# A delta-rule recurrence feeding a two-layer MLP: triangular inverses in 16x16 blocks, joined by small TensorE products

## The chip, the cores and the metric

The kernel runs on one core of one Trainium2 chip. The metric is the device time of one execution in microseconds (us), as a median of several executions. Engines are named as the profile names them: PE is TensorE (matrix products), PEld its weight loads, DVE is VectorE, ACT is ScalarE, POOL is GpSimd, SP issues DMAs. "Fast" and "slow" are the two states that executions fall into; only fast ones are compared.

## The reference, cut to what matters

```python
# q, k, v, beta, g: batch 4, 8 heads, 768 tokens, head size 48
k_n = k / (norm(k) + 1e-6)
for t in range(S):
    y[t] = g[t] * (q[t] @ state)                  # read before the update
    state += beta[t] * outer(k_n[t], v[t] - k_n[t] @ state)
h = x @ w_in                                      # x = y, 3072 tokens x 384; w_in 384 x 2048
out = softplus(h) @ w_out                         # w_out 2048 x 384
```

The recurrence is worked in chunks of 64 tokens. Within a chunk the update is a triangular system, (I + beta L) u = beta (v - k S), with L the strictly lower part of k k^T. The kernel inverts its diagonal blocks and multiplies.

## The kernel before: the parts that matter here

The whole program is a list of items with an engine, a cost estimate, dependencies and a priority. A small planner simulates the engines and emits the instructions in the order that it finds, so each engine has a fixed queue. There are six super-steps (`cc`) of 128 tokens. Each has a preparation (norms, transposes, k k^T, the inverse), a recurrence (two chunks in sequence) and the MLP ("MoE" below) of 512 rows.

```python
# the inverse: one 32x32 block per lane (128 lanes), column by column, on GpSimd
def step(eng, tr_, j, c0, c1, nn=nn, tt=tt):
    n, w = HC - 1 - j, c1 - c0                    # HC = 32: 31 dependent steps
    tmp = tr_.ap[:, : n * w].rearrange("p (i c) -> p i c", c=w)
    eng.tensor_tensor(tmp, nn.ap[:, j+1:, j:j+1].broadcast_to([P, n, w]),
                      tt.ap[:, j:j+1, c0:c1].broadcast_to([P, n, w]), ALU.mult)
    eng.tensor_tensor(tt.ap[:, j+1:, c0:c1], tt.ap[:, j+1:, c0:c1], tmp, ALU.add)
# ... cut: in super-step 0 the columns are split between DVE and GpSimd ...
nc.scalar.copy(t16.ap, tt.ap)                                          # to fp16
nc.vector.transpose(td.ap.rearrange("p u i -> p i u"), t16.ap)         # to TensorE's layout

# k k^T, per head and half: three small products, each with its own weights
nc.tensor.matmul(o[ra, :, h, :], ka, x.ap[r, h, 0, :])
nc.tensor.matmul(o[rb, 0, h, :], kb_, kb_)
nc.tensor.matmul(o[rb, 1, h, :], kb_, ka)

# the inverse applied: 32x32 products, first for all four quarters, then again for two
for h in range(H):
    for qd in parts:                              # (0, 1, 2, 3), later (1, 3)
        r = slice(32 * qd, 32 * qd + 32)
        nc.tensor.matmul(hd(up.ap)[r, h], td_.ap[r, gi * H + h, :], o.ap[r, h])
```

Each `matmul` call becomes two PE instructions, a weight load and a product.

## Time and profile before

| | before |
|---|---|
| time, median | 397.4 us |
| products on PE | 6088 |
| PE busy | 258.4 us |
| GpSimd busy | 235.2 us |
| first recurrence with an inverse | 75.2 us |
| first MoE product | 111.7 us |

Busy time is what an engine executes, whether or not anybody waits for it. The chain of waits is read from the last instruction backwards and says what set the end: half of it is GpSimd. The prediction below shows these lines and reads them. It is the queue of DMAs that bring instructions (number, megabytes, share of 16 DMA engines' time):

```profile
q8 instruction: 47, 0.77, 0.8%
```

0.77 MB in 47 transfers is 16 KB each.

### The profile page before, as it was taken

The numbers are of one execution on the slowest core, as the hardware profiler recorded it, in microseconds if no ns is written. First come the engines' busy times: TensorE is split into PE (matmuls) and PEld (weight loads), VectorE is DVE, ScalarE is ACT, GpSimd is POOL, SyncE is SP. The second block draws the span as 40 slices with busy tenths as digits, with TensorE's granted clock in tenths as the row PEclk, the third lists the DMA queues.
The fourth block names the chain that finished last, engine by engine and source line by source line (L and its number), as shares of the span: only waits on it lengthen the run. The fifth ranks groups of instructions, "written<-read, shape, count | busy, mean of one in ns | idle before, by whom it ended". The sixth has DMA issues, their size and how long they took to land.

```text
span 395.2 us, 13701 instructions
## 1 busy us (share of the span) xinstructions
PE 258.4 (65%) x6088; PEld 163.3 (41%) x6088; DVE 184.8 (47%) x344; ACT 133.5 (34%) x224; POOL 235.2 (60%) x396
## 2 busy tenths in 40 slices
PE   0052100387598169599699648889549999289985
PEld 0042100376543147364266235665225654056442
DVE  1141898969420388651464059742065540254011
ACT  0331001363436243416521357332434217211630
POOL 2440484428888938888888874888813888400000
PEclk9999999999999759959899959898955999779999
DMA  3699876156650046462045031253000010011002
GB/s 71 118 184 183 154 144 119 39 108 123 121 104 0 13 95 130 84 121 53 2 97 125 24 61 27 55 114 72 9 2 3 23 48 14 2 30 34 22 20 61
DMA packets 108634, 27.71 MB, mean 70 GB/s; under 512 B 103072, under 2 KB 108192, under 8 KB 108576
## 3 DMA queue, kind: packets, MB, share of 16 engines
q1 hardware_dynamic: 105216, 23.61, 30.5%
q0 software_dynamic: 2464, 3.15, 4.7%
q8 instruction: 47, 0.77, 0.8%
q10 hardware_dynamic: 896, 0.10, 0.2%
q14 instruction: 11, 0.09, 0.1%
HBM read 25.26 MB, written 4.72 MB: 76 GB/s over the span
## 4 chain that ended last, share of the span: by engine, by line
POOL 51%; DVE 19%; PE 16%; issue 9%; ACTq 3%; DMA 1%; ACT 1%; POOLq 0%; DVEq 0%
POOL tt L544 22%; POOL tmp L538 20%; POOL ss L335 6%; PE o L856 6%; DVE td L617 5%; PE h L824 4%; DVE tmpv L538 3%; DVE tt L544 3%; ACTq L235 3%; POOL nn L511 2%; DVE ln L499 2%; PE d L388 2%; DVE kn L352 1%; DVE ss L322 1%; DVE mt L481 1%
## 5 line engine op out<-in xcount | busy, mean ns | idle before, releaser
L538 POOL TENSOR_TENSOR tmp<-nn,tt 128x31 f32<-128x31 f32 (+23 forms) x178 | 87.7, 493 | 33.1 <-DVE nn L511 19.3
L544 POOL TENSOR_TENSOR tt<-tt,tmp 128x31 f32<-128x31 f32 (+23 forms) x178 | 92.9, 522 | 13.9
L856 PE MATMUL o<-w_out,ga 128*128 128x384 f16 x384 | 81.4, 347 | 9.4 <-ACT ga L838 6.4
L824 PE MATMUL h<-xt,w_in 128*128 128x512 f16 x288 | 78.0, 407 | 2.7 <-DVE xt L778 1.3
L838 ACT ACTIVATE ga<-h 128x512 f16<-128x512 f32 x96 | 56.8, 597 | 64.1 <-PE h L824 62.0
L335 POOL TENSOR_TENSOR ss<-ss,half_c 128x16 f32<-128x16 f32 x12 | 35.0, 2920 | 31.3 <-DVE ss L322 31.2
L856 PEld LDWEIGHTS <-ga 128*128 128x128 f16 x384 | 36.4, 102 | 36.5 <-issue 8.1
L667 PE MATMUL d<-w,td 32*32 32x48 f16 x1152 | 19.3, 193 | 48.6 <-DVE ss L342 37.2
L388 PE MATMUL d<-ident,kn 64*64 64x64 f16 x384 | 14.1, 230 | 51.2 <-DVE kn L352 50.8
L824 PEld LDWEIGHTS <-w_in 128*128 128x128 f16 x288 | 28.0, 101 | 38.9 <-issue 14.4
L676 ACT CAST u<-d 128x384 f16<-128x384 f32 x48 | 21.9, 481 | 59.1 <-PE d L667 59.0
L617 DVE STREAM_TRANSPOSE td<-t 128x1024 f16<-128x1024 f16 x6 | 27.9, 4646 | 28.1 <-ACT t L608 28.1
L667 PEld LDWEIGHTS <-td 32*32 32x32 f16 x1152 | 14.6, 98 | 57.2 <-DVE ss L342 37.5
L408 ACT COPY kqt<-d 128x1024 f16<-128x1024 f16 x24 | 23.7, 1012 | 33.3 <-PE d L388 33.2
L388 PEld LDWEIGHTS <-kn 64*64 64x64 f16 x384 | 11.5, 142 | 53.6 <-DVE kn L352 52.8
L659 DVE TENSOR_TENSOR w<-vf,d 128x384 f16<-128x384 f32 x48 | 25.5, 546 | 13.2 <-PE d L684 12.3
L342 DVE TENSOR_SCALAR ss<-ss 128x16 f32<-128x16 f32 x12 | 3.7, 307 | 59.0 <-POOL ss L335 59.0
L869 DVE COPY osb<-o 128x384 f32<-128x384 f32 x24 | 13.5, 564 | 34.4 <-PE o L856 34.4
L481 DVE TENSOR_TENSOR mt<-d,mask 128x512 f16<-128x512 f32 x24 | 16.0, 685 | 19.6 <-PE d L461 19.4
L309 ACT ACTIVATE ksq<-kf 128x384 f32<-128x384 f32 x24 | 12.0, 522 | 34.6 <-DMA kf<-in_k_dram 31.0
L511 POOL TENSOR_TENSOR nn<-ln,nbeta_l 128x1024 f32<-128x1024 f16 x5 | 9.6, 1913 | 15.2 <-DVE ln L499 15.1
L444 ACT CAST kk<-d 128x512 f16<-128x512 f32 x24 | 13.6, 588 | 14.3 <-PE d L428 14.3
(54 smaller groups left out, 362.9 us busy)
## 6 DMA issues: line engine op xcount, KB each, us to landing
kf<-in_k_dram SPq DMA_DIRECT2D x48, 96.0 KB
qf<-in_q_dram SPq DMA_DIRECT2D x48, 96.0 KB
vf<-in_v_dram SPq DMA_DIRECT2D x48, 96.0 KB
gf<-in_g_dram SPq DMA_DIRECT2D x48, 96.0 KB
out_dram<-osb SPq DMA_DIRECT2D x48, 96.0 KB
w_in<-in_moe_w_in_dram POOLq DMA_DIRECT2D x1, 1536.0 KB, 11.3
w_out<-in_moe_w_out_dram POOLq DMA_DIRECT2D x1, 1536.0 KB, 21.7
beta_l<-in_beta_dram ACTq DMA_DIRECT2D x16, 6.0 KB
```

Source lines behind the costliest of these rows:

```text
L335: nc.gpsimd.tensor_tensor(ss.ap, ss.ap, half_c, ALU.pow)
L388: nc.tensor.transpose(o[r, h, j, :], a.ap[r, h, :], ident[r, r])
L408: lambda tp=tp, o=kqt[gi]: nc.scalar.copy(o.ap.rearrange("p h j t -> p (h j t)"), f16ps(tp.ap))
L538: eng.tensor_tensor(tmp, nn.ap[:, j + 1 :, j : j + 1].broadcast_to([P, n, w]), tt.ap[:, j : j + 1, c0:c1].broadcast_to([P, n, w]), ALU.mult,)
L544: eng.tensor_tensor(tt.ap[:, j + 1 :, c0:c1], tt.ap[:, j + 1 :, c0:c1], tmp, ALU.add)
L617: lambda t16=t16, td=td: nc.vector.transpose(td.ap.rearrange("p u i -> p i u"), t16.ap)
L659: nc.vector.tensor_tensor(o.ap, vf.ap, hd(wp.ap), ALU.subtract)
L667: nc.tensor.matmul(hd(up.ap)[r, h], td_.ap[r, gi * H + h, :], o.ap[r, h],)
L676: nc.scalar.copy(o.ap, hd(up.ap))
L824: nc.tensor.matmul(hp.ap, w_in[:, j, f * P : (f + 1) * P], xt.ap[:, j, :], start=(j == 0), stop=(j == 2),)
L838: lambda hp=hp, o=gb_: nc.scalar.activation(o.ap, hp.ap, AF.Softplus)
L856: nc.tensor.matmul(op.ap[:, :DM], ga[f].ap[:, 128 * gi : 128 * gi + 128], w_out[:, f, :], start=(f == 0), stop=(f == NF - 1),)
```

## The change

The intent is to take the inverse off the critical path. Blocks of 16x16 need 15 steps instead of 31 and a quarter of the elements. The lower left quarter of each 32x32 inverse is then made by TensorE: T21 = -T22 L21 T11. The transpose to TensorE's layout is done in fp32 with contiguous writes. Loads of the inputs are twice as large and half as many, beta is loaded by GpSimd's queue instead of ACT's, and the first super-step takes its square roots on ACT. The pairing of batches and the priorities of the items change too.

```diff
-        def step(eng, tr_, j, c0, c1, nn=nn, tt=tt):
-            n, w = HC - 1 - j, c1 - c0
+        def step(j, tmp=tmp, nn=nn, tt=tt, eng=eng):
+            n, w = 15 - j, j + 1
+            t = tmp.ap[:, : 2 * n * w].rearrange("p (b i c) -> p b i c", b=2, c=w)
             eng.tensor_tensor(...)               # both 16x16 blocks of a lane in one instruction
...
+        def ttr(t32=t32, tt=tt):                 # fp32 transposes, contiguous output
+            for b in range(2):
+                c0 = 16 - 16 * b
+                nc.vector.transpose(
+                    t32.ap[:, 16 * b : 16 * b + 16], tt.ap[:, b, :, c0 : c0 + 32])
...
+        def nat(...):                            # T11 transposed back: 128 products
+            for u in range(U):
+                for qd in range(4):
+                    r = slice(32 * qd, 32 * qd + 32)
+                    nc.tensor.matmul(uv(np_.ap)[r, u], td.ap[r, u, :],
+                                     ident[r, 32 * qd : 32 * qd + 16])
+        def xmm(...):                            # L21 T11: 128 products
+                    r = slice(32 * qd, 32 * qd + 16)
+                    nc.tensor.matmul(uv(xp.ap)[32 * qd : 32 * qd + 32, u],
+                                     kk.ap[r, 0, u, :], tn.ap[r, u, :])
+        def tmm(...):                            # add -T22 X: 4 + 128 products
+                    nc.tensor.matmul(uv(ep.ap)[32 * qd : 32 * qd + 16, u],
+                                     xs.ap[r, u, :], td.ap[r, u, 16:], start=False, ...)
...
-    r_k = ring("kf", 4, [P, H, D], F32)
+    r_k = ring("kf", 3, [P, 2, H, D], F32)      # loads of 192 KB instead of 96 KB
...
-                    nc.scalar.dma_start(out=beta_l[l0 : l0 + 8], ...)      # 16 of them
+                nc.gpsimd.dma_start(out=beta_l[l0 + cl : l0 + 32 : 2], ...)  # 8
...
-        pl = 100 * cc - 200                      # preparation
+        pl = 100 * cc - 70
```

## The prediction

> **What bounds the kernel now.** I read the page first (busy shares, tenths, chain of waits), then the busy time by stretch, then the timelines of GpSimd and of the first 76 us, then the TensorE instructions one by one.
>
> The page, busy time and the chain that ended last:
>
> ```profile
> PE 258.4 (65%) x6088; PEld 163.3 (41%) x6088; DVE 184.8 (47%) x344; ACT 133.5 (34%) x224; POOL 235.2 (60%) x396
> ...
> PE   0052100387598169599699648889549999289985
> ...
> POOL 2440484428888938888888874888813888400000
> PEclk9999999999999759959899959898955999779999
> ...
> POOL 51%; DVE 19%; PE 16%; issue 9%; ACTq 3%; DMA 1%; ACT 1%; POOLq 0%; DVEq 0%
> ```
>
> PE has the most busy time, yet the chain runs for half of the span on GpSimd. The groups of instructions say with what (count, busy us, mean ns):
>
> ```profile
> L538 POOL TENSOR_TENSOR tmp<-nn,tt 128x31 f32<-128x31 f32 (+23 forms) x178 | 87.7, 493 | 33.1 <-DVE nn L511 19.3
> L544 POOL TENSOR_TENSOR tt<-tt,tmp 128x31 f32<-128x31 f32 (+23 forms) x178 | 92.9, 522 | 13.9
> ...
> L335 POOL TENSOR_TENSOR ss<-ss,half_c 128x16 f32<-128x16 f32 x12 | 35.0, 2920 | 31.3 <-DVE ss L322 31.2
> ...
> L617 DVE STREAM_TRANSPOSE td<-t 128x1024 f16<-128x1024 f16 x6 | 27.9, 4646 | 28.1 <-ACT t L608 28.1
> ```
>
> There are six super-steps of 128 tokens. Each needs the triangular inverses of 128 blocks of 32x32, one to a lane: 31 dependent column steps of two instructions. In the GpSimd timeline the inverses of super-steps 1 to 5 start at 94, 150, 190, 248 and 305 us and the last ends at 341.8: some 50 us apart, of which one inverse is 37.7 (94.1 to 132.0), the two powers 5.8, the scaling of N 1.9 and clearing T 1.2, together 46.6. So the middle is GpSimd-bound. Two more parts are not: a head, until super-step 0 has gone through the recurrence, and a tail after 341.8. Busy time by stretch (window, length, then PE, PEld, DVE, ACT, POOL with counts, clock, DMA share, GB/s):
>
> ```profile
> 0.00:42.00 42.00, 9.81 (x416) 8.64 (x416) 11.15 (x38) 9.05 (x13) 11.66 (x17) 1.00 0.84 144
> 42.00:75.00 33.00, 0.00 (x0) 0.00 (x0) 30.84 (x70) 2.52 (x4) 21.45 (x49) 1.00 0.60 114
> ...
> 303.00:342.00 39.00, 34.32 (x532) 18.89 (x528) 11.11 (x23) 11.96 (x22) 33.99 (x63) 0.94 0.09 22
> ```
>
> In the second stretch PE does nothing: the first inverse runs, split between DVE and GpSimd (44 to 68.6), then a 1.0 us cast and the 4.6 us transpose. The first recurrence starts at 75.2 and the first MoE product only at 111.7 (timeline of PE). The first 14 us look like this:
>
> ```profile
> 0.81 12.36 ACTq L235 DMA_DIRECT2D beta_l<-in_beta_dram  x16
> ...
> 14.49 1.76 ACT L309 ACTIVATE ksq<-kf 128x384 f32<-128x384 f32 x4
> ```
>
> The first half of k had landed at 5.5 us (k is the first 4096 packets of the SP queue; the 2048th ended there), but ACT was issuing beta loads until 13.2.
>
> **What the Trainium skill says.** (1) "GPSIMD Engine Reference", section 3.1 Elementwise: a two-input elementwise instruction costs software dispatch plus about 2.6 cycles per element. The trace agrees in form: a line through 183 start-to-start times of the column steps gives 0.281 us plus 1.82 ns per element. Halving the work therefore does not halve the fixed part unless the count falls too. (2) "TensorE: Matmul & The Clock Gate", Part 3, The mechanism: 32x32 tiles of the array overlap, a few ns apart. The trace agrees: 64 products of 32x32 (w,td) take 0.83 us at half clock and 32 take 0.38 us at full, so about 9 ns each. (3) The same page, "What's actually happening": an idle window of about 3.4 us drops the clock to half. The trace agrees: after the idle 283 to 289 us three h products take 1.46 us, against 0.81 warm. A PE with fewer idle gaps will also be a faster PE. (4) "ScalarE: Activation LUTs", What ACT_TABLE_LOAD costs: 1283 ns; the two loads here show exactly 1283. The new Sqrt in super-step 0 adds a switch.
>
> **The change part by part.**
>
> *Inverse on GpSimd.* Blocks shrink to 16x16, two to a lane and both in one instruction: 15 steps, 30 instructions, with 2 x sum of (15-j)(j+1) = 1360 elements each for multiply and add, 2720 in all. By the line above: 30 x 0.281 + 2720 x 0.00182 = 8.4 + 5.0 = 13.4 us (the same line gives 37.3 for the old form, measured 37.7). Two preps of 256: 1.5 us. Clear and diagonal: about 0.8. One power over 32 columns instead of two over 16: 5.8, unchanged, as it scales with columns (2.92 for 16). Sum 21.5 us against 46.6 per super-step. GpSimd falls to about 5 x 21 plus the start, some 120 us: no bound.
>
> *First inverse, all on DVE.* The DVE steps of the old one fit 0.178 us + 2.1 ns per element: 30 x 0.178 + 2720 x 0.0021 = 11.1 us, against 24 now. Saves 13 in the head.
>
> *Transpose.* One fp16 transpose with scattered 2-byte writes, 4.65 us, becomes two fp32 ones of 512 elements with contiguous output. The ln transpose, with contiguous output, is 1.9 us for 1024 elements, so at most 1 us each; I take 1.4 for both. DVE loses 3.2 us per super-step, 20 in all. The ACT cast stays, 1.05.
>
> *The join, new.* nat 128, xmm 128, tmm 132 products per super-step. At 9 ns: 1.2 + 1.2 + 1.4 = 3.8 us of PE, 23 us over six, and three ACT evictions of 512 columns at about 0.59 (as the kk row) = 1.8 us, 11 us over six. As latency: 1.4 + 1.05 + (1.4 + 0.6) x 2 + 1.6 + 0.6 and some 1.2 of hand-overs = 10 us, about what cast, transpose and waits take now (66 or 68.6 to 75.2).
>
> *Loads.* Same bytes, same 192 B packets, half the issues: no bandwidth gained, and the DMA share is low after 112 us. Beta leaves ACT for GpSimd: eight software DMAs at about 1 us (the two weight loads show 0.97 and 1.19). They stand ahead of the identity on GpSimd, and the DVE queue starts with the identity cast, then the memsets. So the first reduce waits until about 12.5 instead of 15.6: a gain of 3, not 8. Sqrt on ACT replaces two 2.9 us powers there.
>
> *Head, added up.* First reduce 12.5; sqrt, reciprocal, scale: first kn at about 15.5 and second at 17 (20.6 and 26.1 now). Transposes, kqt and kk copies (ACT 4 x 1.0 + 4 x 0.59 = 6.4) and the "issue" gaps of PE under heavy DMA load (3.2 and 4.2 us now, I keep about 5): kk complete near 30 (40.4 now). ln 1.9, preps 0.8, steps 11.1: 44. Join 10: the recurrence starts at about 54, against 75.2. The recurrence of a super-step alone took 19 us late in the trace (347.6 to 366.5), 36 in the head, where it waited for powers and k of the next; I take 22. The first MoE product starts at about 76, against 111.7: **36 us gained in the head.**
>
> *After the head PE is the bound.* Work at full clock: MoE 288 x 0.216 + 384 x 0.163 = 124.8 us (medians of the start-to-start times). Small products: the 64-row ones at 16.5 ns, the 32-row ones at 9 to 10, transposes of y at 66: 73.9 us. Join 23. Total 222, of which prep 0 and 1, recurrence 0 and join 0, 5 + 5 + 7.6 + 3.8 = 21, fall into the head. Left: 201 us. No stretch runs at 100%: by the same accounting 305 to 337 us had 0.87 of its time in such work, 248 to 282.5 had 0.79, 194 to 227 had 0.75, each with a full queue of MoE work but half-cold clock in the latter two. With the clock warm more often I take 0.85: 201 / 0.85 = 236. The last copy and store add 2 to 3. Sum: 76 + 236 + 2 = **314 us.**
>
> **The rivals.** (a) *GpSimd still bounds*: the 16x16 steps cost more than the line says, as every access now has one more dimension. At double, 27 + 8 = 35 us per super-step, still below PE's 37 / 0.85 = 43. Time 320 to 330. Speaks against: the line fits short and long steps alike. (b) *The chain through the join bounds*: k, norm, power 5.8, transposes, ln, 15 us of GpSimd, 10 us of join is some 45 us per super-step, with five PSUM banks shared by prep, join and recurrence. If it isn't overlapped with the super-step before, PE idles and cools as now: 340 to 365. For it: in-order queues planned from estimates, five banks only. Against: k, kn and kqt have room for more than two super-steps, and preparation has only to fit into gaps of PE. (c) *DVE or ACT bound*: DVE falls to 185 - 13 - 20 + some 5 = 157, ACT rises to 145; both are half of 314, so no. (d) *The MoE tail and the recurrence chain are denser than I think*: at 0.92, 218 us, time 296.
>
> **Range and chances.** Density 0.78 to 0.92 moves the sum by about plus or minus 20; the head by plus or minus 8. Range 292 to 338. For the change to stay within 2%, 83 us of gain would have to vanish although GpSimd's half of the chain is cut by more than half: 2% for same, 1% for slower, 97% for faster.
>
> **What would show it right or wrong.** GpSimd steps: 30 per super-step, about 13.4 us from first to last; GpSimd busy near 120 us. First recurrence product near 54 us and first MoE product near 76. Join: PE bursts of 128 in about 1.2 us. The two fp32 transposes below 1 us each. The chain of waits led by PE, with GpSimd below 15%; PE busy above 75% of the span; mean clock above 0.92. Wrong: if the chain still names GpSimd, or if PE shows gaps over 3 us in the middle that wait on td or on a PSUM bank (rival b); if beta or the identity holds DVE past 15 us; or if a strided ACT copy or the fp32 transposes take several us.

## The result, and the profile after

The changed kernel takes 363.6 us (median of 4 executions, 362.6 to 369.7; the longest is a slow one, and the three fast ones have the median 363.0), against 397.4. The ratio is 0.914, with a 95% interval of 0.911 to 0.917. Ratios here are the mean time of one kernel's fast runs over that of the other's in the same rounds, so they are not quite the ratio of the medians quoted. It is faster, as forecast, but by 34 us and not by 83; 363.6 lies well outside 292 to 338.

The page of the changed kernel, in the same rows as before:

```profile
PE 274.1 (76%) x8416; PEld 175.7 (49%) x8416; DVE 148.1 (41%) x280; ACT 148.9 (41%) x233; POOL 104.5 (29%) x196
...
PE   0351035669996897779999978985899978999984
...
POOL 6400060054830892000528987000006600000000
PEclk9985555555997599569999998995599998999999
...
q8 instruction: 65, 1.06, 1.3%
...
PE 71%; issue 13%; DVE 7%; ACT 5%; SPq 2%; DMA 1%; DVEq 0%; ACTq 0%
```

GpSimd has left the chain altogether, and PE carries it, as predicted. Two entries don't fit. "issue", time in which an engine waited for nothing that the profile shows, is 13% of the chain, 47 us. And the clock row has a long stretch of fives, half clock, near the start, where the kernel before had nines. The groups behind the prediction's steps:

```profile
L582 POOL TENSOR_TENSOR tt<-tt,tmp 128x30 f32<-128x30 f32 (+7 forms) x75 | 29.5, 393 | 5.9
L575 POOL TENSOR_TENSOR tmp<-nn,tt 128x30 f32<-128x30 f32 (+7 forms) x75 | 28.7, 382 | 5.9
...
L368 POOL TENSOR_TENSOR ss<-ss,half_c 128x32 f32<-128x32 f32 x5 | 27.4, 5487 | 59.7 <-DVE ss L329 59.7
...
L609 DVE STREAM_TRANSPOSE t<-tt 128x512 f32<-128x512 f32 x12 | 7.7, 684 | 0.0
```

The inverse is as cheap as predicted. On the other engines the promise was kept. The busy time by stretch shows where it was not (columns as in the prediction: PE and PEld busy with their counts, then DVE, ACT, POOL, the clock, the DMA share, GB/s):

```profile
0.00:57.00 57.00, 13.63 (x808) 11.70 (x808) 30.00 (x73) 16.92 (x21) 16.26 (x26) 0.71 0.95 162
57.00:88.00 31.00, 22.70 (x908) 20.31 (x909) 13.81 (x23) 11.95 (x18) 7.31 (x6) 0.50 0.55 105
...
142.00:158.00 16.00, 10.02 (x463) 6.77 (x464) 4.35 (x8) 5.54 (x8) 0.00 (x0) 0.54 0.69 135
158.00:195.00 37.00, 35.99 (x1038) 22.44 (x1037) 20.63 (x36) 20.17 (x35) 11.39 (x14) 0.97 0.32 63
...
241.00:258.00 17.00, 9.46 (x584) 7.68 (x584) 3.22 (x8) 3.82 (x6) 0.00 (x0) 0.64 0.31 63
295.00:347.00 52.00, 48.94 (x1028) 26.91 (x1025) 10.52 (x21) 22.67 (x41) 0.00 (x0) 0.97 0.11 25
```

In 57 to 88, 142 to 158 and 241 to 258 us PE executes almost only small products, gets through one per 29 to 35 ns (31 us / 908, 16 / 463, 17 / 584), and every other engine is mostly idle. The stretches with MoE products in them (158 to 195, 295 to 347) are full. The timeline of PE at the first join shows what the small products wait for (start, duration, instruction, count, idle before and its releaser):

```profile
46.69 1.19 PE L637 MATMUL d<-ident,td 32*32 32x16 f16 x128 [15.44 <-ACT td L618]
48.75 0.65 PE L657 MATMUL d<-tn,kk 16*32 16x16 f16 x63 [0.86 <-ACT tn L647]
51.52 0.66 PE L657 MATMUL d<-tn,kk 16*32 16x16 f16 x65 [2.12 <-issue]
...
52.92 0.59 PE L691 MATMUL d<-td,xs 32*16 32x16 f16 x59 [0.29 <-ACT xs L668]
55.52 0.67 PE L691 MATMUL d<-td,xs 32*16 32x16 f16 x69 [2.00 <-issue]
```

The 128 products of one item run at 9 ns each, as predicted, and then PE stops in the middle of the next item, after 63 of 128 products, for 2.1 us, with all data there. It does so again after 59 of 128 in the item after that. From 46.69 to 48.75 and on to 51.52 it had executed 128 + 63 = 191 products, and between the two breaks 65 + 4 + 59 = 128. With the weight loads that is 256 instructions. The instruction queue made 65 transfers of 16 KB for 16832 PE instructions (8416 products and as many loads), one for every 259. In the trace those transfers start at 48.5, 52.7 and 56.6 us here; the shortest distance between two starts in the run is 3.3 us.

A count over the whole trace, with loads and products in order of start, says the same: of the 24 gaps over 1 us between PE instructions, 20 come after 191 + 256n instructions, at one and the same place of a page, and these 20 last 40.7 us together. The kernel before had its two "issue" gaps in the head at such places too, after 447 and 703 instructions (191 + 256 and 191 + 512).

**Theory A**: PE's instructions arrive in pages of 256, at most one page per 3.3 to 4 us, so by an estimate from these distances a load-and-product pair costs some 26 to 31 ns in supply, whatever its size. Long products hide this (16 of them last 3 us and are 32 instructions); the join doesn't. **Theory B**, a rival: PE runs at the array's pace and loses time because the clock is at half, 0.83 on average. **Theory C**, another: the chain of one super-step through join and recurrence sets the time.

### The profile page after: what moved, and what is told of

It reads as the page before. It is cut to its first block, busy times and chain, and to the rows that moved or that the text cites. A ratio compares the mean times of both kernels' runs of the same rounds, so it can differ in the third digit from the quotient of the medians.

```text
span 362.2 us, 17913 instructions
## 1 busy us (share of the span) xinstructions
PE 274.1 (76%) x8416; PEld 175.7 (49%) x8416; DVE 148.1 (41%) x280; ACT 148.9 (41%) x233; POOL 104.5 (29%) x196
## 4 chain that ended last, share of the span: by engine, by line
PE 71%; issue 13%; DVE 7%; ACT 5%; SPq 2%; DMA 1%; DVEq 0%; ACTq 0%
PE o L940 19%; PE h L908 19%; PE d L436 5%; PE d L752 4%; PE d L732 2%; PE d L504 2%; SPq L262 2%; ACT td L618 2%; PE d L657 2%; PE d L470 2%; PE d L637 2%; PE d L691 2%; PE d L813 2%; PE d L790 2%; PE d L824 2%
## 5 line engine op out<-in xcount | busy, mean ns | idle before, releaser
L908 PE MATMUL h<-xt,w_in 128*128 128x512 f16 x288 | 80.8, 410 | 0.8 <-DVE xt L863 0.4
L940 PE MATMUL o<-w_out,ga 128*128 128x384 f16 x384 | 75.5, 336 | 4.8 <-DVE osb L953 4.2
L922 ACT ACTIVATE ga<-h 128x512 f16<-128x512 f32 x96 | 56.8, 598 | 52.7 <-PE h L908 51.1
L368 POOL TENSOR_TENSOR ss<-ss,half_c 128x32 f32<-128x32 f32 x5 | 27.4, 5487 | 59.7 <-DVE ss L329 59.7
L908 PEld LDWEIGHTS <-w_in 128*128 128x128 f16 x288 | 25.5, 102 | 27.6 <-issue 8.0
L953 DVE COPY osb<-o 128x384 f32<-128x384 f32 x24 | 13.4, 557 | 55.7 <-PE o L940 55.7
L582 POOL TENSOR_TENSOR tt<-tt,tmp 128x30 f32<-128x30 f32 (+7 forms) x75 | 29.5, 393 | 5.9
L575 POOL TENSOR_TENSOR tmp<-nn,tt 128x30 f32<-128x30 f32 (+7 forms) x75 | 28.7, 382 | 5.9
L564 POOL TENSOR_TENSOR nn<-ln,nbeta_l 128x256 f32<-128x256 f16 x10 | 6.0, 619 | 67.4 <-DVE ln L541 67.4
L752 PEld LDWEIGHTS <-td 32*32 32x32 f16 x1152 | 14.4, 96 | 18.2 <-issue 15.3
L637 PE MATMUL d<-ident,td 32*32 32x16 f16 x768 | 7.4, 172 | 19.2 <-ACT td L618 17.7
L799 DVE TENSOR_TENSOR s<-d,s 128x384 f16<-128x384 f32 x22 | 12.0, 553 | 16.4 <-PE d L790 16.4
L637 PEld LDWEIGHTS <-td 32*32 32x32 f16 x768 | 6.7, 90 | 20.8 <-ACT td L618 18.5
```

Of the source, the lines that this page charges most:

```text
L368: lambda ss=ss: nc.gpsimd.tensor_tensor(ss.ap, ss.ap, half_c, ALU.pow)
L575: eng.tensor_tensor(t, nn.ap[:, :, j + 1 :, j : j + 1].broadcast_to([P, 2, n, w]), tt.ap[:, :, j : j + 1, 16 : 16 + w].broadcast_to([P, 2, ...
L582: eng.tensor_tensor(rows, rows, t, ALU.add)
L637: nc.tensor.matmul(uv(np_.ap)[r, u], td.ap[r, u, :], ident[r, 32 * qd : 32 * qd + 16],)
L752: nc.tensor.matmul(hd(up.ap)[r, h], td_.ap[r, u0 + 2 * h, :], o.ap[r, h],)
L908: nc.tensor.matmul(hp.ap, w_in[:, j, f * P : (f + 1) * P], xt.ap[:, j, :], start=(j == 0), stop=(j == 2),)
```

## The experiments

All runs are against the kernel before on the same chip; differences below are between medians over all executions and the 363.6 us of the changed kernel, which ran only in the first comparison. The changed kernel, e3, e9 and e14 each have one slow execution among four; with fast ones alone their medians are 363.0, 364.2, 329.7 and 330.3, and no difference below moves by more than 0.6 us. Up to run e8, the kernel before took 397.0 us, in e9 to e12 397.9 and in e13 and e14 397.8.

**e1: supply measured alone.** A kernel of products without waits between them, with a wrong result.

```python
for i in range(2048):                       # t32: four row tiles in turn
    nc.tensor.matmul(ps[n][r, c : c + 16], a[r, :32], a[r, 32:48])
for i in range(2048):                       # t64: two row tiles in turn
    nc.tensor.matmul(ps["t64"][r, c : c + 64], a[r, :64], a[r, 64:128])
for i in range(64):                         # mix
    t32("mix", 16); big("mixb", 2)          # big: 128x128, 512 columns
# 60 big ones before, between and after
```

> A wrong result on purpose: only TensorE products, no waits between them. 2048 products of 32x32 (16 columns), then 2048 of 64x64 (64 columns), then 64 times 16 small ones followed by two of 512 columns, with runs of 512-column products between. Theory A (instruction supply: TensorE gets its instructions in pages of 256, and a page takes at least 3.3 us in the trace of the changed kernel): both small stretches settle at one page, 128 load-and-product pairs, per 3.3 to 3.5 us, so 26 to 27 ns per product whatever its size, some 54 us each, with gaps that nothing but issue ends; the mixed stretch is bound by its products, about 0.58 us per 18, 37 us, without gaps. Theory B (my prediction: the array's own pace, only slowed by the half clock): 9 ns and 16.5 ns per product, 18 and 34 us.

The timeline of PE, two pieces of it, 32x32 products first and 64x64 products then:

```profile
46.64 1.19 PE L35 MATMUL t<-a 32*32 32x16 f16 x128 [2.53 <-issue]
50.65 1.19 PE L35 MATMUL t<-a 32*32 32x16 f16 x128 [2.81 <-issue]
54.37 1.19 PE L35 MATMUL t<-a 32*32 32x16 f16 x128 [2.54 <-issue]
```

```profile
98.61 2.21 PE L44 MATMUL t<-a 64*64 64x64 f16 x128 [0.84 <-issue]
102.34 2.21 PE L44 MATMUL t<-a 64*64 64x64 f16 x128 [1.52 <-issue]
```

After a start with more pairs in hand, 163 in the first piece and 231 in the second, PE executes exactly 128 pairs, then stops, then 128 pairs. The first 2048 took 63.0 us (15.93 to 78.95), 30.8 ns each; the second 2048, with four times the columns and twice the rows, 59.0 us (93.92 to 152.96), 28.8 ns each. The period from burst to burst, once settled, is 3.7 to 4.0 us in the first piece and 3.4 to 4.0 in the second, somewhat longer than I had expected. The transfer of one page takes only 0.9 to 1.5 us of it in this trace; what the rest is stays open. In the mixed stretch no gap of this kind was left, but it took 46.7 us (166.0 to 212.7), not the 37 expected: a group of 16 small and 2 long products lasts 0.73 us instead of 0.58. The clock fell to half at 21 us, after the stops had begun at 17, and stayed there until 83, which is the stretch in which PE stood still two thirds of the time. In the second piece it was 0.91 on average, and the pace was nearly the same. Theory A holds for supply; Theory B fails for streams of small products. Every execution lists a granted clock, so each was probably profiled; whether the profiler itself slows the supply, no run tests.

**e2: the back-transpose issued twice, and e3: long products instead.** Both add array time to the join; e2 with many instructions, e3 with few.

```diff
-            for u in range(U):
+            for u in list(range(U)) * 2:                      # e2, in nat
```
```diff
         def xmm(kk=kk, tn=tn, xp=xp, uv=uv):
+            for _ in range(6):                                # e3
+                nc.tensor.matmul(xp.ap, ident, kk.ap.rearrange("p x u t -> p (x u t)")[:, :512])
```

> The 128 products that transpose the inverse back are issued twice, to the same place: 6 x 128 more products, 6 more pages of instructions, 1.2 us of array work each. Theory A (supply): most of a page per super-step is exposed, since the join stands where no long products run: +13 to +21 us. Theory B (array pace, half clock): +7 us (+1.2 us in each of six super-steps).

> Six products of 128x128x512 (result thrown away) ahead of xmm in each super-step: 1.3 us of array work at full clock, 2.6 at half, but only 12 instructions each. Theory A (supply): the page that xmm waits for is fetched meanwhile, so most of it fits into gaps that are there anyway: 0 to +4 us. Theory B: +8 to +15 us, more than in the run with nat twice.

e2 took 383.1 us, 19.5 more: 25 ns for each of the 768 added products. e3 took 364.4 us, 0.8 more, although it adds as much array time (6 x 1.3 us) as e2 adds in theory B. In its profiled execution the first stop inside `xmm` comes exactly six products earlier than in the changed kernel, after 57 instead of 63, because the six long products take their place in the page; and the stop is shorter, as the long products run meanwhile:

```profile
47.90 2.74 PE L655 MATMUL d<-kk,ident 128*128 128x512 f16 x6
50.57 0.60 PE L663 MATMUL d<-tn,kk 16*32 16x16 f16 x57
51.80 0.71 PE L663 MATMUL d<-tn,kk 16*32 16x16 f16 x71 [0.63 <-issue]
```

The long products also kept the clock up, 0.957 on average against 0.83. That makes e3 a test of theory B in place: between the first inverse and the first MoE product its clock was 1.00, against 0.50 in the changed kernel, and the same 908 small products took 30 us instead of 31:

```profile
57.00:87.00 30.00, 22.97 (x908) 20.35 (x909) 13.96 (x24) 11.85 (x18) 7.65 (x7) 1.00 0.58 108
```

All these results are those of theory A.

**e4: half of the first U products.** The second pass writes quarters 1 and 3 anew, so the first pass needs only 0 and 2. Two long products with zero weights fill the rest.

```diff
+                    for qd in (1, 3) if fill else ():
+                        nc.tensor.matmul(up.ap[r, : H * D], zero_w[r], o.ap[r].rearrange("p h d -> p (h d)"))
...
-                f(o, (0, 1, 2, 3))
+                f(o, (0, 2), True)
```

> The first product with the inverse only for the two quarters whose result is used; the other two quarters are filled with zeros by two products of 384 columns. 14 fewer products per chunk, 336 in all, with the same array time (two of 384 columns side by side in place of 16 of 48). Theory A (supply): 672 instructions less, 2.6 pages, about -9 us (-5 to -11). Theory B (array pace, half clock): 0, within 1 us.

359.5 us, -4.1. This is below the range that I had set for theory A, and outside that of B. A likely reason, not tested by itself, is that these products stand among MoE products, which hide part of their supply.

**e5: two products instead of three for k k^T**, the second one writing its halves in reverse order.

```diff
-                            nc.tensor.matmul(o[rb, 0, h, :], kb, kb)
-                            nc.tensor.matmul(o[rb, 1, h, :], kb, ka)
+                            nc.tensor.matmul(o[rb, ::-1, h, :], kb, x.ap[r, h, 0, :])
```

> The two 32-column products of each second half of k against k become one of 64 columns, written with the halves in reverse order: 16 products fewer per chunk, 384 in all, 768 instructions, 3 pages; the array streams as many columns as before. Theory A (supply, 3.9 us per page in the run of products alone): 3 pages x 3.9 = 11.7 us if all were exposed; the run with half the first U products showed that less than half of it was, so -4 to -9 us, more than there, as a third of these products lies in the head where nothing hides them. Theory B (array pace, clock): 0 to -1 us.

357.5 us, -6.1: within A, outside B, though the array streams as many columns as before. The four executions also test the clock by themselves: 355.7 and 357.2 us at 0.932 and 0.936, 357.9 and 359.7 at 0.837 and 0.832. A tenth of the clock goes with 2.4 us here. In e4 the order is the reverse: the fastest execution, 357.8 us, had 0.841, and the others, 359.5 to 360.5, had 0.92. So the low mean clock of the changed kernel can explain a few us, not fifty.

**e6: the back-transpose on VectorE.** The 128 products of `nat` go; a third fp32 transpose and an ACT copy make the same tile.

```diff
-        def nat(np_=np_, td=td, uv=uv): ...
+        def ntr(n32=n32, tt=tt):
+            nc.vector.transpose(n32.ap, tt.ap.rearrange("p b i c -> p c (b i)")[:, 16:32, :])
+        ... nc.scalar.copy(tn.ap, n32.ap.rearrange("p j u -> p u j"))
```

> The 128 products that transpose the 16x16 inverse back are left out; one fp32 transpose of 512 elements on VectorE straight from the rows of the inverse, and an ACT copy of 512 elements, take their place. 768 products, 1536 instructions, 6 pages fewer. Theory A: as doubling them cost 19.5 us (3.2 per page), leaving them out gains 15 to 23 us: 341 to 349 us. Theory B: -7 us of products, +3 us for the strided ACT copy: 358 to 361 us.

350.2 us, -13.4. This lies between the two ranges and nearer A's. By e2 the removed products should be worth some 19.5; that the copy and a new order of the queue give back the rest is likely, but was not tested. Theory B alone allowed -3 to -6.

**e7: the old inverse with everything else of the change.** No join; 31 steps on GpSimd.

> The changed kernel with the 32x32 inverse of before on GpSimd (first one split with VectorE as before), no join; new loads, beta on GpSimd's queue, Sqrt in the first super-step, the fp32 transpose stay. TensorE has the instructions of the kernel before, 18 pages fewer than the changed one. Both theories: GpSimd bounds again, five rounds of about 50 us; head shorter by 12 to 18 us than in the kernel before: 372 to 390 us. If it is below 364, the change of the inverse was a loss.

416.3 us, slower than the kernel before (ratio 1.049). I had expected 372 to 390. The head was shorter, as expected: the first inverse started at 34.4 us instead of 44.2. But GpSimd then had to wait; its waits in this run, and for whom (us in total, times, longest); the same two waits add up to 15.1 and 31.2 us in the kernel before:

```profile
POOL nn L554 <- DVE ln L542: 47.4, 3, 25.4
POOL ss L369 <- DVE ss L330: 33.2, 3, 17.7
```

The likely reason is the lower priority of the preparation, which belongs to the change: the next super-step's k comes to GpSimd late, which matters only where GpSimd is the bound. No run changed the priority alone. So this run does not isolate the loads. It shows that the rest of the change brings no gain with the long inverse, and that at this order the new inverse with its join is worth 53 us (416.3 against 363.6).

**e8: the kernel before with the cuts of e4 and e5.**

> The kernel before with the same two cuts of TensorE instructions (half the first U products, two products instead of three for k against k): 720 products, 5.6 pages fewer. Theory A: the kernel before is bound by GpSimd, so the pages are mostly hidden there: -1 to -7 us (within 2%). A rival to A, that such cuts gain the same everywhere because they shorten the chain of products itself, says -8 to -16 us, as the sum of the two cuts in the changed kernel.

391.7 us, -5.3 (ratio 0.987), against -10.2 for the sum of the two cuts in the changed kernel. Where GpSimd is the bound, the same cut gains half as much.

**e9: the three cuts together** (e4, e5 and e6).

> The three cuts of TensorE instructions together: half the first U products, two products for k against k, back-transpose on VectorE. 1488 of 8416 products left out, 11.6 pages. Theory A (supply), if the gains add: -4.1 - 6.1 - 13.4 = -23.6 us, 340 us (335 to 346). If another bound stands close behind (the chain of one super-step, or the array itself), clearly less: 347 to 353.

329.9 us, ratio to the kernel before 0.828 (0.826 to 0.830), correct. That is 33.8 us below the changed kernel, 10 more than the three gains add up to; why more is not settled (the planner finds another order when items change). It beats both kernels. From its page:

```profile
PE 256.7 (78%) x6928; PEld 163.9 (50%) x6928; DVE 152.4 (47%) x287; ACT 149.5 (46%) x233; POOL 104.3 (32%) x196
...
q8 instruction: 54, 0.88, 1.1%
...
PE 68%; issue 9%; DVE 8%; ACT 4%; POOL 4%; DMA 3%; SPq 3%; ACTq 0%; DVEq 0%
```

PE has less to do by 17 us busy time, and "issue" in the chain fell from 13% of 362 us to 9% of 327, from 47 to 29 us.

**e10, e11 and e12: another order.** e10 leaves the instructions of the changed kernel as they are, and makes the planner charge PE for supply. e11 adds that to e9. e12 adds to e11 a head in which the identity comes before the beta loads and the clearing of tiles moves to GpSimd.

```diff
+                left_now = min(384.0, have + (t0 - seen) * 67.37)      # instructions in hand
...
-                    key=lambda x: (x[1].prio, x[1].n),
+                    key=lambda x: ((x[1].ins - left_now) / 67.37 > 0.2, x[1].prio, x[1].n),
```

> The changed kernel with the same instructions; only their order is planned anew: the planner charges TensorE 3.8 us per 256 instructions with 384 in hand, and places long MoE products, where they are ready, ahead of a burst whose instructions would not have come. Theory A: gaps that issue ends fill with MoE work: 345 to 358 us. Rival C (the chain of one super-step sets the time and supply only stretches it): delaying chain products behind MoE costs as much as it gains: 361 to 372 us.

> Both: three cuts and the order planned with supply. Theory A: 322 to 337 us. If order does nothing: as the three cuts alone, near 340.

> As the run with cuts and order, and in the head the identity and masks come before the beta loads on GpSimd, the clearing of the inverse's tiles moves from VectorE to GpSimd, and the negated beta is made later, so that the first sum of squares does not wait on VectorE's queue (11.25 us now, k squared at 7.95). Gain 2 to 4 us if the head counts fully: 319 to 334 us.

e10 took 367.8 us, 4.1 more than the changed kernel. e11 took 331.3 and e12 332.7, each about as e9 or slower. None of the three gained. In e10 the first MoE product came 4 us earlier (84.7 instead of 88.7) and the end later, so what was pulled forward was lost behind. Its chain had less "issue" than the changed kernel's, 10% against 13%, and yet it took longer:

```profile
PE 72%; issue 10%; DVE 7%; ACT 4%; DMA 3%; SPq 2%; ACTq 0%; DVEq 0%
```

This is what rival C had said of e10, and my expectation of A for the order was wrong: supply can be saved by having fewer instructions, but this way of hiding it did not work. So C is not refuted: the page waits may cost what they do because they lengthen the chain of one super-step. A better planner might help; that stays open. The head's queue on VectorE (e12) was worth nothing.

**e13 and e14: the join without its instructions.** All 388 products of the join are replaced by 3 or by 18 long ones with zero weights, in the same places, with the same evictions, waits and PSUM banks. T21 is then zero, which is wrong (the comparison with the reference still passed its tolerance, so for these inputs that check does not see T21).

```diff
-            for u in range(U):
-                for qd in range(4): ...                        # 128, 128 and 132 products
+            for _ in range(1):                                 # e13; 6 in e14
+                nc.tensor.matmul(np_.ap, zero_w, td.ap.rearrange("p u i -> p (u i)")[:, :512])
```

> A wrong result on purpose: the join's 388 products per super-step become 3 long ones of 512 columns with zero weights, in the same places; its evictions, waits and PSUM banks stay. So the time against the changed kernel is what the products themselves cost. My prediction's step (array pace, 9 ns each): 23 us less 6 x 0.65 = -19 us. Theory A (supply; 19.5 us per 768 products as the run with nat twice showed, 2328 products): -55 to -60 us if that price holds for all, and not below the 314 us predicted with the join in: 304 to 325 us.

> The same with 18 long products, 3.9 us of array work per super-step at full clock, what I had charged the join with, but 36 instructions instead of 776. Theory A: array work costs at most its own time, 6 x 3.3 = +20 us over the run with 3, less where it keeps the clock up: 310 to 338 us, far below 363.6. Theory B (array time is what counts): within 5 us of the changed kernel, 358 to 369.

e13 took 316.3 us, 47.3 less than the changed kernel. e14 took 330.3 us (326.1 to 330.4 in its fast runs), 33.3 less, though it keeps 3.9 us of array work per super-step, what I had charged. The gap between the two, 14 us, is 6 x 3.3 us of array work, partly hidden. The gap between e14 and the changed kernel, 33 us, is what 740 instructions per super-step cost beyond their array time, in the same order of queues and with the same waits. Like A, C allows this result, as fewer instructions also shorten the chain; B had said 358 to 369 us and fails.

## Why the prediction was wrong, by its own steps

- *GpSimd leaves the chain; its steps.* Right. The 15 steps took 13.1 to 14.8 us from first to last (predicted 13.4), the power 5.5 (5.8), GpSimd was busy 104.5 us (near 120), and its share of the chain is nil. The fp32 transposes took 0.68 us each (1.4 for both).
- *First inverse and head up to the inverse.* Right within a few us. The first reduce started at 11.25 us (12.5), the steps on DVE took 8.7 (11.1), and they ended at 43.3 (44).
- *"The ACT cast stays, 1.05".* Wrong, and small: 1.97 us. It now reads with a stride of 128 bytes where the old cast read in order; shape and types are the same. It costs 0.9 us of latency in each super-step.
- *"At 9 ns: 1.2 + 1.2 + 1.4 = 3.8 us of PE, 23 us over six".* **This is the step that failed.** 9 ns is the pace of a burst whose instructions are already there, and I had read it from bursts of 32 and 64. The pace that lasts is 29 to 31 ns (e1), and in place 25 ns per added product (e2). Taking the join's products away gained 47 us (e13), where the prediction had 19 us of array time, or 22 with its density of 0.85, to gain by that edit. That is about 25 of the 50 us that were missing.
- *"The recurrence of a super-step ... I take 22. The first MoE product starts at about 76."* Recurrence products with the inverse did start at 57.0 (54), but MoE only at 88.7. In the 31 us between there were 908 small products, 34 ns each, and e3 took 30 us for them at full clock. I had read the gaps named "issue" in the head of the kernel before, 3.2 and 4.2 us long, as an effect of DMA load that would stay at 5 us. They were page waits (after 447 and 703 instructions, as above). This is 13 us. It overlaps with the join: in e13 the first MoE product came at 82.0, so 6.7 of the join's 47 us lie in the head, where the prediction had charged some 3.2; about 4 us are counted in both steps.
- *"I take 0.85".* The same accounting gives 0.73 after 88.7 us (199 us of array work in 273). The reasons that I gave for a higher density, a warmer clock and no wait for GpSimd, were of the wrong kind: I had taken 0.75 to 0.87 from stretches rich in MoE products, whose length hides supply. I had also called the clock of the two less dense ones half-cold, and the trace shows 0.90 and 0.95 there. What is left of the miss beyond join and head, about 16 us (50 - 25 - 13, plus the 4 counted twice), is in line with the supply of the older small products (e4 and e5 gained 10 us there with no array work saved), but it was not isolated.
- *The clock.* Predicted above 0.92, measured 0.83. The mechanism (idle PE cools) was right: in e1 the clock fell to half 4 us after the stops began. Its sign was not, since the new idle gaps came from supply. It matters little, as e3 and the executions of e4 and e5 show.
- *Rivals.* (b) had the right symptom, PE idling inside preparation and join, and the wrong cause: neither td nor a PSUM bank was what most of the long gaps waited for (20 of the 24 over 1 us stand at the page's end; the longest, 15.7 us in the head, did wait for the first td). No rival named the supply of instructions.
- *Direction and chances.* Faster by over 2% was right, and for the reason given, GpSimd's exit from the chain; the size was not.

## What to carry to other kernels

Count the instructions of an engine, not only its busy time: here the change moved work from a slow engine into hundreds of tiny TensorE products, whose array time was cheap (23 us charged) and whose instruction supply was not. When "issue" appears in the chain at regular distances of 128 products, replace small products by fewer or longer ones, or do the step on an engine with room, before working on clock or order. A pace read from a short burst holds for what is already fetched, so take it from a stretch longer than two pages.

## What the Trainium skill lacked or had wrong

- "Runtime: NRT & Kernel Launch", section Instruction fetch mechanics, has the block of 256 instructions right, but says that crossing into the next block is mostly hidden. Here it was not hidden: a block of 128 load-and-product pairs lasts 1.2 us in execution at 32x32 and comes every 3.7 to 4.0 us (e1), and the changed kernel had 40.7 us of gaps at the ends of blocks.
- "TensorE: Matmul & The Clock Gate", sections Back-to-back issue gap and Part 3, gives about 25 ns as the issue floor for products of 1 to 64 columns and a few ns between tiles. Bursts over row tiles went below that floor here, with 9 ns over four tiles and 17 ns over two (2.21 us for 128), and the lasting pace was above it, 29 to 31 ns. I found nothing there of a lasting pace that is nearly the same for 32x32 with 16 columns and 64x64 with 64 (they differ by 7%).
- "SBUF — State Buffer" warns that strided reads pay a penalty, but no page that I found gives a figure for an ACT copy: 1024 fp32 elements per lane to fp16 took 1.97 us with a stride of 128 bytes and 1.04 in order.
